# Emptying the finished accumulators at a change of tile: when it is done, and in how many pieces

## The chip, the cores and the metric

One core of a Trainium2 chip. The metric is the device time of one execution in microseconds, the median of the runs. The engines are PE (TensorE), VectorE (DVE in the profile), ScalarE (ACT), GpSimd (POOL) and the DMA queues, SP's above all.

## The reference

```python
w = softmax(weight, axis=-1)             # 8 heads, 7 taps
out[b, s, h, g] = sum_k w[h, k] * x[b, s + k - 6, h, g]   # causal convolution, 24 channels a head
x = out.reshape(16384, 192)
x = (maximum(x @ w_in, 0) ** 2) @ w_out          # layer 1, 192 -> 2048 -> 192
h = x @ w_in2
x = maximum(0.01 * h, h) @ w_out2                # layer 2, 192 -> 2048 -> 192
```

All in float32: 4 x 4096 tokens of 192 channels, a short convolution, and two feed-forward layers one after the other.

## The kernel before

**Tiles and steps.** The 16384 tokens are 32 tiles of 512. A unit (l, t) is layer l on tile t. The units run in the order of `phases` (L297): the pair (1,0) and (1,1) with their steps in turn, then (1,2), (1,3), the pair (2,0) and (2,1), (2,2), (2,3), and from then on, for t = 4, 6, ..., four units: (1,t), (1,t+1), (2,t), (2,t+1). A unit has 8 steps, one for each pair p of 128-column chunks of the 2048; 512 steps in all.

**A step.** PE computes two chunks `h` of the hidden layer (`g1`, L552), ScalarE makes `g` of them by the activation (`act`, L572), in layer 1 one of the two squares is taken on ScalarE and the other on VectorE from step 16 on (`square`, L580), ScalarE casts `g` to a rounded high part `hi` (`high`, L598), VectorE subtracts to get the low part `lo` (`low`, L605), and from step 48 on VectorE also adds the two `lo` of a step to `both` (`add_low`, L611), which saves matmuls. Two steps later (LAG = 2) PE multiplies these with the second weights into accumulators (`g2_one`, L712, through `paired`, L685; for the pairs of tiles `g2`, L631). Matmuls have 64 rows; the two halves of the array run two at a time, each on its own accumulator.

**The accumulators.** 192 output channels in 128-column blocks give a single tile three banks: M (the main 128), F and E, of which half by half the sums are put together: the output's first 128 channels are `M` plus, on one half of the partitions, the other half of `E`, and on the other half the other half of `F`; the last 64 channels are one half of `F` plus the other half of `E`. There are four banks for these (`tags`, L621). The next tile takes the fourth for its M at once, the old E for its F and the old F for its E, so its first matmuls need the old E and F emptied, and the old M only a tile later. In the last step of a tile PE ends E first, then F and M.

**Emptying** (`evac_one`, L732; `evac`, L825, for a pair). `early` (L741) has ScalarE copy E in two copies of 64 partitions, each to the other half: one to `z3`, one to `zs`, a tile of its own. `other` (L746) has ScalarE copy half of F across to `z3`. `add_rest` (L749) adds on VectorE F's other half and `zs`. `add_main` (L752) adds on VectorE M and `z3` on 128 partitions. Then `then` holds what follows three steps on: splitting the sums into the next layer's operand (layer 1), or transposing and storing them (layer 2).

**The order of the work** is written out in a schedule by hand; each engine runs its instructions in the order in which the loop over s (L1160) issues them. In step s PE's part comes first. In step s with p = 1 the last `g2` of the tile before is issued, `leaving` holds the emptying and `alone` is true for a single tile. `early` then stands ahead of the two activations (L1228), `other` and `add_rest` behind the squares (L1268 to L1269), `add_main` at the end (L1280). For a pair all of it stands at the end of the step (L1283).

**Fill.** The convolution (7 taps on VectorE for each 512 tokens and block, L430), decoding the weights (`dec`), splits and transposes (`leave`) are pieces with a cost and a due time. `pieces(s, left)` (L1054) takes them between the step's own instructions: at most `many` a step (2, in layer 1 three, and 1 in the step after a change of tile), and only while `budget` is positive or the piece is due. The budget grows by 3880 a step (4100 before step 48) less the step's own cost, and is at most 4100.

Of the kernel before, what the change touches and what calls it, by code (L numbers as in the profile page):

```python
# [11 lines left out]
I32 = mybir.dt.int32  # L12
# [6 lines left out]
P = 128  # L19
TT = 512  # L20
# [3 lines left out]
LAG = 2  # L24
# [39 lines left out]
def conv_moe_moe2_kernel(  # L64
# [10 lines left out]
    nc = tc.nc  # L75
# [5 lines left out]
    NP = NF // 2  # L81
# [6 lines left out]
    NW = NI + NO  # L88

    const = ctx.enter_context(tc.tile_pool(name="const", bufs=1))  # L90
    stage = ctx.enter_context(tc.tile_pool(name="stage", bufs=1))
# [640 lines left out]
    def evac_one(u):  # L732

        l, t = u
        (M, m_tag), (F, f_tag), (E, e_tag) = ops.pop(u)
        tags.extend([e_tag, f_tag, m_tag])
        v, w = halves(t % 2), halves(1 - t % 2)
        z, z3, zr = ring[:, 0, :], ring[:, 1, :], ring[:, 2, :]
        got = {}

        def early():  # L741
            got["s"] = f32(stage.tile([P, NW], I32, tag="m", name="zs")[:, 0:TT])
            nc.scalar.copy(out=z3[w], in_=E[v])
            nc.scalar.copy(out=got["s"][v], in_=E[w])  # L744

        def other():  # L746
            nc.scalar.copy(out=z3[v], in_=F[w])  # L747

        def add_rest():  # L749
            nc.vector.tensor_add(out=zr[v], in0=F[v], in1=got["s"][v])  # L750

        def add_main():  # L752
            nc.vector.tensor_add(out=z, in0=M, in1=z3)

        if l == 1:
            b, a = splits((2, t), lambda: z, lambda: zr)
            then = [k + ((2, t),) for k in b + a]
        else:
            then = []
            y = y_of(t)  # L760

            def main():
                nc.vector.transpose(out=y()[:, t % 2], in_=z)
                for j in range(4):
                    store(y(), t % 2, j, t, 32 * j)

            def rest():
                nc.vector.transpose(out=y()[:, 2], in_=zr)
                for j in range(4):
                    store(y(), 2, j, t - 1 + j // 2, P + 32 * (j % 2))  # L770

            def rest_alone():
                nc.vector.transpose(out=y()[v, 2], in_=zr[v])
                for j in range(2):
                    store(y(), 2, 2 * (t % 2) + j, t, P + 32 * j)

            then.append((700, main, None, None))
            if t == NT - 2:
                then.append((700, rest_alone, None, None))
            elif t % 2:  # L780
                then.append((700, rest, None, None))
        return (early, other, add_rest, add_main), then

    ys = {}

# [16 lines left out]
    def evac_last(u):  # L802

        l, t = u
        (early, other, add_rest, add_main), _ = evac_one(u)
        early()
        other()
        add_rest()
        add_main()
        v = halves(t % 2)  # L810
        z, zr = ring[:, 0, :], ring[:, 2, :]
        dmas = [nc.sync, nc.scalar]
        y = stage.tile([P, 3, TT], F32, tag="y", name="y").rearrange("p k t -> p (k t)")[:, 0:4 * D].rearrange("p (k d) -> p k d", d=D)
        for i in range(2):
            turned = ps_h.tile([P, TT], F32, tag="h", name="turned")[:, 0:2 * D].rearrange("p (k d) -> p k d", d=D)
            for k in range(2):
                at_ = slice(P * (2 * i + k), P * (2 * i + k + 1))
                nc.tensor.matmul(out=turned[:, k, 0:P], lhsT=z[:, at_], rhs=ident, start=True, stop=True)
                nc.tensor.matmul(out=turned[:, k, P:D], lhsT=zr[v, at_], rhs=ident[v, v], start=True, stop=True)
            w = y[:, 2 * i:2 * i + 2]  # L820
            (nc.vector.tensor_copy if i else nc.scalar.copy)(out=w, in_=turned)
            r0 = t * TT + 2 * P * i
            dmas[i].dma_start(out=out[r0:r0 + 2 * P, :].rearrange("(k t) d -> t k d", t=P), in_=w)

    def evac(u):  # L825

        l, q = u
        o = ops.pop(u)
        tags.extend(tag_of[u][k] for k in ((0, "m"), (1, "m"), (0, "r"), (1, "r")))
        T = [2 * q, 2 * q + 1]  # L830
        z = {}

        def take(i):
            z[i] = ring[:, i, :]
            (nc.vector.tensor_copy if i else nc.scalar.copy)(out=z[i], in_=o[i, "m"])  # L835

        def shift(i):
            if i == 0:
                z["s"], z["r"] = f32(stage.tile([P, NW], I32, tag="m", name="zs")[:, 0:TT]), ring[:, 2, :]
            nc.scalar.copy(out=z["s"][halves(i)], in_=o[i, "r"][halves(1 - i)])  # L840

        def add(i):
            v = halves(i)
            nc.vector.tensor_add(out=z["r"][v], in0=o[i, "r"][v], in1=z["s"][v])

        now = [(0, lambda: take(0)), (690, lambda: take(1))]
        for i in range(2):
            now += [(0, lambda i=i: shift(i)), (690, lambda i=i: add(i))]
        if l == 1:
            then = []  # L850
            for i in range(2):
                b, a = splits((2, T[i]), lambda i=i: z[i], lambda: z["r"])
                then += [p + ((2, T[i]),) for p in a + b]
            return now, then

        y = y_of(2 * q)

        def main(i):
            nc.vector.transpose(out=y()[:, i], in_=z[i])
            for j in range(4):  # L860
                store(y(), i, j, T[i], 32 * j)

        def rest():
            nc.vector.transpose(out=y()[:, 2], in_=z["r"])
            for j in range(4):
                store(y(), 2, j, T[j // 2], P + 32 * (j % 2))

        return now, [(700, lambda: main(0), None, None), (700, lambda: main(1), None, None), (700, rest, None, None)]

    with tc.manual_schedule():  # L870
# [77 lines left out]
        def decode_one():  # L948
            cost, fn = dec.popleft()[1:3]
            fn()  # L950
            budget[0] -= cost
            return cost
# [178 lines left out]
        def needed(s, n):  # L1131

            while n > 0 and dec and dec[0][4] <= s:
                n -= decode_one()
            return n
# [18 lines left out]
            return [g1(u, p), 9]  # L1154

        prep_next = 2
        late = []
        left_at = -2
        going = begin_g1(0)
        for s in range(NS):  # L1160
# [43 lines left out]
            cost = (2100 if vector else 1400) + (700 if three else 0)  # L1204
            budget[0] = max(min(budget[0] + (SHORT if three else STEP) - cost, STEP), DEBT)
            many = MANY[l - 1] + (l == 1 and s >= 4 * NP or 2 * NP - 4 <= s < 2 * NP) if s > 1 else 4
            if left_at == s - 1:
                many = 1
            if leaving:
                left_at = s  # L1210
# [1 line left out]
            if s < 2 * NP:  # L1212
                play(s, A, Z)
                late = [Z]
                if s == 0:
                    split_a((1, 2), third)
                    split_a_lo((1, 2), third)
                continue
            if leaving:
                while leave:  # L1220
                    z = leave.popleft()
                    z[2]()
                    release()
                    budget[0] -= max(z[1], 0)
                while dec and getattr(dec[0][2], "second", False):
                    decode_one()
                if alone:
                    leaving[0]()  # L1228
            left = [many, 1]
            if u in in_pair:  # L1230
                act(*A)
                if late and late[0] not in hi:
                    high(*late[0])
                if not alone:
                    needed(s, 10000)
                    pieces(s, left)
                while leaving and not alone and dec and getattr(dec[0][2], "second", False):
                    decode_one()
                if l == 1:
                    square(*A, False)  # L1240
                if alone:
                    leaving[1]()
                    leaving[2]()
                    leaving[3]()
                    needed(s, 10000)
                    pieces(s, left)
                if late:
                    low(*late.pop())
                high(*A)
# [3 lines left out]
            else:  # L1253
# [5 lines left out]
                act(*one)  # L1259
                act(*two)  # L1260
                needed(s, 10000)
                if not (alone and dec):
                    pieces(s, left, 700)
                if l == 1:
                    square(*Z, vector)
                    square(*A, False)
                if alone:
                    leaving[1]()  # L1268
                    leaving[2]()  # L1269
                pieces(s, left)  # L1270
                while leaving and not alone and dec and getattr(dec[0][2], "second", False):
                    decode_one()
                high(*one)
                high(*two)
                low(*one)
                low(*two)
                if three:
                    add_low(u, p)
                if alone:
                    leaving[3]()  # L1280
                    budget[0] -= 1400
            if leaving and not alone:
                for c, fn in leaving:  # L1283
                    fn()
                    budget[0] -= c
            release()
            if u in in_pair and l == 1:
                square(*Z, vector)
# [40 lines left out]
```

## Time and profile before

| | |
|---|---|
| median of 3 runs | 2165.09 us (2159.32 to 2166.94) |
| the profiled execution | 2162.51 us |
| its span, first to last instruction | 2160.8 us |
| PE busy | 2084.4 us (96% of the span) |
| VectorE busy | 1648.7 us (76%) |
| ScalarE busy | 1478.4 us (68%) |
| GpSimd busy | 60.1 us (3%) |
| mean granted clock of TensorE | 0.995 |

The span is the traced time of one execution; 1.7 us of the execution lie around it. Busy time is the union of an engine's instructions; PE's counts matmuls as pipelined, so its share says little of how far it is from its peak, and the length of a step says more.

### The profile page before, as it was taken

To read this page: it belongs to the slowest core of one execution; us is meant where nothing else is said; L and a number is where in the kernel's file an instruction comes from. 1 tells how busy PE (TensorE), PEld (TensorE's weight loads), DVE (VectorE), ACT (ScalarE), POOL (GpSimd) and SP (SyncE) were. 2 spreads that over 40 slices of the span, in tenths; PEclk is the share of its full clock that TensorE was granted. 3 is DMA by queue.
4 is the path that set the end of the run, shared out by engine and by line. 5 is a ranking of instruction groups with operands and counts; after the bars stand their busy time and mean duration, and the time that the engine had idled before them with its cause. 6 is when DMAs were issued, how large, how long until landed. Compare 5 with 4: busy or idle time off the path is not lost.

```text
span 2160.8 us, 47005 instructions
## 1 busy us (share of the span) xinstructions
PE 2084.4 (96%) x18592; PEld 1974.9 (91%) x18592; DVE 1648.7 (76%) x2575; ACT 1478.4 (68%) x2700; POOL 60.1 (3%) x114
## 2 busy tenths in 40 slices
PE   9899999999999999999999999999999999999998
PEld 6789998999999899998999999999998999989997
DVE  8877678787787877778777787877778777787664
ACT  7877567667676666767667676676767667677674
POOL 2201110000000000000000000000000000000000
PEclk9999999999999999999999999999999999999999
DMA  8540131121212112131121211212121121311110
GB/s 191 137 108 21 27 54 26 39 37 45 37 24 46 29 45 40 21 65 26 36 38 32 50 26 38 37 44 38 24 50 26 45 41 21 64 26 35 25 31 16
DMA packets 232677, 95.07 MB, mean 44 GB/s; under 512 B 203208, under 2 KB 218696, under 8 KB 232456
## 3 DMA queue, kind: packets, MB, share of 16 engines
q1 hardware_dynamic: 229288, 88.90, 21.0%
q0 software_dynamic: 1168, 2.75, 0.6%
q8 instruction: 145, 2.38, 0.5%
q14 instruction: 76, 0.62, 0.1%
q10 hardware_dynamic: 2000, 0.42, 0.1%
HBM read 25.19 MB, written 12.58 MB: 17 GB/s over the span
## 4 chain that ended last, share of the span: by engine, by line
PE 65%; DVE 17%; ACT 11%; issue 5%; DMA 1%; SPq 0%; DVEq 0%; ACTq 0%
PE h L544 31%; PE o1m L544 12%; PE o0r L544 11%; PE o1r L544 7%; DVE lo L607 5%; PE o0m L544 4%; ACT hi L603 2%; DVE g L583 2%; DVE acc_b L435 2%; DVE ring L750 2%; ACT g L576 2%; DVE acc_a L435 2%; ACT ring L747 2%; ACT zs L744 2%; ACT g L578 2%
## 5 line engine op out<-in xcount | busy, mean ns | idle before, releaser
L544 PE MATMUL h<-x,w 64*128 64x512 f32 x9216 | 1362.9, 377 | 2.6 <-ACT g L578 1.4
L544 PEld LDWEIGHTS h<-x,w 64*128 64x128 f32 x9216 | 1067.5, 186 | 13.8 <-ACT g L578 1.8
L607 DVE TENSOR_TENSOR lo<-g,hi 128x512 fp32r<-128x512 f32 x1022 | 661.8, 688 | 347.1 <-ACT hi L603 289.7
L603 ACT CAST hi<-g 128x512 fp32r<-128x512 f32 x1020 | 580.9, 619 | 134.5 <-DVE g L583 130.8
L544 PE MATMUL o1m<-hi,w 64*128 64x512 f32 x2044 | 632.6, 385 | 30.5 <-DVE ring L750 28.7
L544 PE MATMUL o0r<-hi,w 64*128 64x512 f32 x1948 | 601.6, 384 | 17.9 <-DVE ring L750 17.9
L578 ACT ACTIVATE g<-h 128x512 f32<-128x512 f32 x512 | 279.6, 595 | 321.3 <-PE h L544 320.5
L544 PEld LDWEIGHTS o1m<-hi,w 64*128 64x128 f32 x2044 | 358.5, 186 | 59.9 <-DVE ring L750 37.7
L544 PEld LDWEIGHTS o0r<-hi,w 64*128 64x128 f32 x1948 | 342.2, 186 | 47.6 <-DVE ring L750 26.2
L544 PE MATMUL o0r<-lo,w 64*128 64x512 f32 (+1 forms) x1022 | 383.5, 378 | 0.4 <-DVE lo L607 0.4
L576 ACT ACTIVATE g<-h 128x512 f32<-128x512 f32 x512 | 278.6, 593 | 139.9 <-PE h L544 138.1
L544 PE MATMUL o1m<-both,w 64*128 64x512 f32 x926 | 352.4, 381 | 8.1 <-DVE both L619 8.1
L619 DVE TENSOR_TENSOR both<-lo 128x512 fp32r<-128x512 f32 x463 | 320.5, 692 | 18.0
L544 PE MATMUL o0m<-hi,w 64*128 64x512 f32 x1088 | 326.9, 380 | 4.4 <-ACT ring L835 3.2
L544 PE MATMUL o1r<-hi,w 64*128 64x512 f32 x1052 | 321.2, 380 | 1.0 <-ACT zs L744 1.0
L544 PE MATMUL o0m<-lo,w 64*128 64x512 f32 x560 | 209.1, 378 | 0.6 <-DVE lo L607 0.5
L544 PEld LDWEIGHTS o0m<-hi,w 64*128 64x128 f32 x1088 | 191.2, 186 | 9.7 <-ACT ring L835 4.0
L544 PE MATMUL o1r<-lo,w 64*128 64x512 f32 (+1 forms) x526 | 198.0, 376 | 0.0
L544 PEld LDWEIGHTS o1m<-both,w 64*128 64x128 f32 x926 | 172.3, 186 | 19.0 <-DVE both L619 16.8
L544 PEld LDWEIGHTS o0r<-lo,w 64*128 64x128 f32 (+1 forms) x1022 | 187.4, 183 | 2.3 <-issue 0.8
L544 PEld LDWEIGHTS o1r<-hi,w 64*128 64x128 f32 x1052 | 186.6, 186 | 2.4 <-ACT zs L744 1.4
L583 DVE TENSOR_TENSOR g<-g 128x512 f32<-128x512 f32 x243 | 165.6, 682 | 20.1 <-ACT g L576 17.4
(136 smaller groups left out, 1337.6 us busy)
## 6 DMA issues: line engine op xcount, KB each, us to landing
x<-x SPq DMA_DIRECT2D x189, 256.0 KB
out_dram<-y SPq DMA_DIRECT2D x186, 64.0 KB
raw_a<-in_x_dram SPq DMA_DIRECT2D x127, 64.0 KB
raw_b<-in_x_dram SPq DMA_DIRECT2D x62, 64.0 KB
lent<-in_moe_w_out_dram SPq DMA_DIRECT2D x13, 256.0 KB
lent<-in_moe_w_in_dram SPq DMA_DIRECT2D x13, 192.0 KB
lent<-in_moe_w_in_dram SPq DMA_DIRECT2D x13, 128.0 KB
lent<-in_moe_w_out_dram SPq DMA_DIRECT2D x13, 128.0 KB
```

Of the source, the lines that this page charges most:

```text
L435: nc.vector.scalar_tensor_tensor(out=acc[0], in0=src, scalar=w, in1=acc[0], op0=ALU.mult, op1=ALU.add)
L544: return nc.tensor.matmul(out=o.rearrange("p (b a) -> p b a", a=2), lhsT=w, rhs=z.rearrange("p (a b) -> p b a", a=2), start=begin, stop=end_,)
L576: nc.scalar.activation(out=g, in_=hps.pop((u, f)), func=ACTF.Relu)
L578: nc.scalar.activation(out=g, in_=hps.pop((u, f)), func=ACTF.Prelu, alpha=0.01)
L583: nc.vector.tensor_mul(out=g, in0=g, in1=g)
L603: nc.scalar.copy(out=a, in_=gsp[u, f])
L607: nc.vector.tensor_sub(out=b, in0=gsp.pop((u, f)), in1=f32(hi[u, f]))
L619: nc.vector.tensor_add(out=c, in0=f32(lo[u, 2 * p]), in1=f32(lo[u, 2 * p + 1]))
L744: nc.scalar.copy(out=got["s"][v], in_=E[w])
L747: nc.scalar.copy(out=z3[v], in_=F[w])
L750: nc.vector.tensor_add(out=zr[v], in0=F[v], in1=got["s"][v])
```

## The change

`early` becomes one ScalarE copy of E on 128 partitions to `z3`, without changing halves; the tile `zs` is gone. `other` copies F's half to `z` instead of `z3`. `add_rest` adds F's half and `z3`'s other half. `add_main` becomes two additions of 64 partitions: M and `z3` of the other half, then M and `z`. So two VectorE additions now take one input from other partitions than they write.

In the step of the change `early`, `other` and `add_rest` stand at its head, ahead of the activations; for a pair all six operations do. `add_main` moves into `then[0]` and is issued at the end of the step. `both` of the step before a change to another single tile (`soon`) is kept in `pending` and issued behind `add_rest`. In the step of the change `many` is 1, the pieces ahead of the squares are left out, and the budget is charged 1400 for pairs too.

```diff
--- before.py
+++ after.py
@@ -736,21 +736,18 @@
         tags.extend([e_tag, f_tag, m_tag])
         v, w = halves(t % 2), halves(1 - t % 2)
         z, z3, zr = ring[:, 0, :], ring[:, 1, :], ring[:, 2, :]
-        got = {}
-
         def early():
-            got["s"] = f32(stage.tile([P, NW], I32, tag="m", name="zs")[:, 0:TT])
-            nc.scalar.copy(out=z3[w], in_=E[v])
-            nc.scalar.copy(out=got["s"][v], in_=E[w])
+            nc.scalar.copy(out=z3, in_=E)
 
         def other():
-            nc.scalar.copy(out=z3[v], in_=F[w])
+            nc.scalar.copy(out=z[v], in_=F[w])
 
         def add_rest():
-            nc.vector.tensor_add(out=zr[v], in0=F[v], in1=got["s"][v])
+            nc.vector.tensor_add(out=zr[v], in0=F[v], in1=z3[w])
 
         def add_main():
-            nc.vector.tensor_add(out=z, in0=M, in1=z3)
+            nc.vector.tensor_add(out=z[w], in0=M[w], in1=z3[v])
+            nc.vector.tensor_add(out=z[v], in0=M[v], in1=z[v])
 
         if l == 1:
             b, a = splits((2, t), lambda: z, lambda: zr)
@@ -779,7 +776,7 @@
                 then.append((700, rest_alone, None, None))
             elif t % 2:
                 then.append((700, rest, None, None))
-        return (early, other, add_rest, add_main), then
+        return (early, other, add_rest), [add_main] + then
 
     ys = {}
 
@@ -802,11 +799,11 @@
     def evac_last(u):
 
         l, t = u
-        (early, other, add_rest, add_main), _ = evac_one(u)
+        (early, other, add_rest), then = evac_one(u)
         early()
         other()
         add_rest()
-        add_main()
+        then[0]()
         v = halves(t % 2)
         z, zr = ring[:, 0, :], ring[:, 2, :]
         dmas = [nc.sync, nc.scalar]
@@ -843,9 +840,7 @@
             v = halves(i)
             nc.vector.tensor_add(out=z["r"][v], in0=o[i, "r"][v], in1=z["s"][v])
 
-        now = [(0, lambda: take(0)), (690, lambda: take(1))]
-        for i in range(2):
-            now += [(0, lambda i=i: shift(i)), (690, lambda i=i: add(i))]
+        now = [lambda: take(0), lambda: take(1), lambda: shift(0), lambda: add(0), lambda: shift(1), lambda: add(1)]
         if l == 1:
             then = []
             for i in range(2):
@@ -1154,7 +1149,7 @@
             return [g1(u, p), 9]
 
         prep_next = 2
-        late = []
+        late, pending = [], deque()
         left_at = -2
         going = begin_g1(0)
         for s in range(NS):
@@ -1204,7 +1199,7 @@
             cost = (2100 if vector else 1400) + (700 if three else 0)
             budget[0] = max(min(budget[0] + (SHORT if three else STEP) - cost, STEP), DEBT)
             many = MANY[l - 1] + (l == 1 and s >= 4 * NP or 2 * NP - 4 <= s < 2 * NP) if s > 1 else 4
-            if left_at == s - 1:
+            if left_at == s - 1 or leaving:
                 many = 1
             if leaving:
                 left_at = s
@@ -1216,6 +1211,7 @@
                     split_a((1, 2), third)
                     split_a_lo((1, 2), third)
                 continue
+            soon = s + 1 >= LAG and steps[s + 1 - LAG][1] == NP - 1 and steps[s + 1 - LAG][0] not in in_pair
             if leaving:
                 while leave:
                     z = leave.popleft()
@@ -1224,26 +1220,20 @@
                     budget[0] -= max(z[1], 0)
                 while dec and getattr(dec[0][2], "second", False):
                     decode_one()
-                if alone:
-                    leaving[0]()
+                for fn in leaving:
+                    fn()
+                budget[0] -= 1400
+            while pending:
+                pending.popleft()()
             left = [many, 1]
             if u in in_pair:
                 act(*A)
                 if late and late[0] not in hi:
                     high(*late[0])
-                if not alone:
-                    needed(s, 10000)
-                    pieces(s, left)
-                while leaving and not alone and dec and getattr(dec[0][2], "second", False):
-                    decode_one()
+                needed(s, 10000)
+                pieces(s, left)
                 if l == 1:
                     square(*A, False)
-                if alone:
-                    leaving[1]()
-                    leaving[2]()
-                    leaving[3]()
-                    needed(s, 10000)
-                    pieces(s, left)
                 if late:
                     low(*late.pop())
                 high(*A)
@@ -1259,30 +1249,21 @@
                 act(*one)
                 act(*two)
                 needed(s, 10000)
-                if not (alone and dec):
+                if not leaving:
                     pieces(s, left, 700)
                 if l == 1:
                     square(*Z, vector)
                     square(*A, False)
-                if alone:
-                    leaving[1]()
-                    leaving[2]()
                 pieces(s, left)
-                while leaving and not alone and dec and getattr(dec[0][2], "second", False):
-                    decode_one()
                 high(*one)
                 high(*two)
                 low(*one)
                 low(*two)
                 if three:
-                    add_low(u, p)
-                if alone:
-                    leaving[3]()
-                    budget[0] -= 1400
-            if leaving and not alone:
-                for c, fn in leaving:
-                    fn()
-                    budget[0] -= c
+                    (pending.append if soon else lambda fn: fn())(lambda u=u, p=p: add_low(u, p))
+            if alone:
+                then[0]()
+                then = then[1:]
             release()
             if u in in_pair and l == 1:
                 square(*Z, vector)
```

## Rows read from the trace of the kernel before

**Rows 1.** The page's first part: busy time, share of the span, instructions.

```profile
PE 2084.4 (96%) x18592; PEld 1974.9 (91%) x18592; DVE 1648.7 (76%) x2575; ACT 1478.4 (68%) x2700; POOL 60.1 (3%) x114
```

**Rows 2.** Who waited for whom on PE: us in total, times, longest.

```profile
PE o1m L544 <- DVE ring L750: 28.7, 30, 2.4
PE o0r L544 <- DVE ring L750: 17.9, 28, 1.0
```

**Rows 3.** Stretches of one step: length, then PE, PEld, DVE, ACT, POOL busy, PEclk, DMA.

```profile
116.24:120.34 4.10, 4.10 (x42) 3.90 (x39) 3.13 (x6) 3.27 (x6) 0.00 (x0) 1.00 0.63 158
101.43:112.14 10.71, 7.45 (x52) 6.17 (x50) 7.87 (x13) 6.39 (x13) 4.57 (x2) 0.84 0.11 24
140.84:151.24 10.40, 7.05 (x41) 5.50 (x39) 6.68 (x11) 4.99 (x9) 0.68 (x2) 0.69 0.81 212
248.41:257.50 9.09, 7.37 (x50) 6.53 (x48) 4.78 (x8) 4.62 (x10) 2.13 (x6) 0.81 0.16 35
1045.92:1049.81 3.89, 3.89 (x40) 3.89 (x38) 3.59 (x6) 2.58 (x6) 0.00 (x0) 1.00 0.01 2
1041.29:1045.92 4.63, 4.32 (x39) 3.79 (x37) 2.45 (x4) 3.77 (x8) 0.00 (x0) 1.00 0.00 0
974.03:979.32 5.29, 4.32 (x39) 3.79 (x37) 4.04 (x7) 4.19 (x8) 0.00 (x0) 1.00 0.01 3
983.21:988.22 5.01, 4.39 (x40) 3.64 (x37) 4.44 (x7) 3.86 (x8) 0.00 (x0) 1.00 0.17 21
1007.87:1014.04 6.17, 4.57 (x39) 3.71 (x37) 5.29 (x9) 4.94 (x10) 0.00 (x0) 1.00 0.00 0
2023.24:2028.53 5.29, 4.32 (x39) 3.79 (x37) 3.25 (x6) 4.19 (x8) 0.00 (x0) 1.00 0.00 0
```

**Rows 4.** Timeline of the change into (2,14): start us, us, engine, line, operation [idle before].

```profile
1040.48 0.58 ACT L743 COPY ring<-o1m 64x512 f32<-64x512 f32 x1 [1.42 <-PE o1m L544]
...
1041.15 0.38 PE L544 MATMUL o0r<-lo,w 64*128 64x512 f32 x1
...
1041.68 1.08 ACT L578 ACTIVATE g<-h 128x512 f32<-128x512 f32 x2
...
1042.79 0.58 ACT L747 COPY ring<-o0r 64x512 f32<-64x512 f32 x1
...
1042.88 0.38 PE L544 MATMUL o1m<-both,w 64*128 64x512 f32 x1
...
1043.40 0.70 DVE L750 TENSOR_TENSOR ring<-o0r,zs 64x512 f32<-64x512 f32 x1 [2.73 <-ACT ring L747]
...
1044.15 0.48 PE L544 MATMUL o0r<-hi,w 64*128 64x512 f32 x1 [0.31 <-DVE ring L750]
```

**Rows 5.** Timeline of VectorE after the change into (1,14) and at that into (1,15).

```profile
981.03 0.69 DVE L753 TENSOR_TENSOR ring<-o1r,ring 128x512 f32<-128x512 f32 x1
...
982.39 0.65 DVE L583 TENSOR_TENSOR g<-g 128x512 f32<-128x512 f32 x1
983.73 1.29 DVE L607 TENSOR_TENSOR lo<-g,hi 128x512 fp32r<-128x512 f32 x2 [0.69 <-ACT hi L603]
985.05 0.69 DVE L619 TENSOR_TENSOR both<-lo 128x512 fp32r<-128x512 f32 x1
...
1008.76 0.69 DVE L619 TENSOR_TENSOR both<-lo 128x512 fp32r<-128x512 f32 x1
```

**Rows 6.** Lines of ScalarE and VectorE (busy us, mean ns | idle), and two timeline rows.

```profile
L835 ACT COPY ring<-o0m 128x512 f32<-128x512 f32 x2 | 1.2, 578 | 0.0
...
L410 DVE COPY xT_a<-xT_a 128x6 f32<-128x6 f32 x26 | 4.4, 168 | 0.0
...
L413 DVE COPY xT_b<-xT_b 64x6 f32<-64x6 f32 x16 | 2.6, 164 | 0.6
...
107.33 0.67 DVE L844 TENSOR_TENSOR ring<-o1r,zs 64x512 f32<-64x512 f32 x1
108.03 0.69 DVE L844 TENSOR_TENSOR ring<-o0r,zs 64x512 f32<-64x512 f32 x1
```

## The prediction

> **What bounds the kernel now.** I read the page's first part, then who waited for whom on PE, then step lengths, then the order of work around three changes of tile. PE is busy 96% of the span, VectorE 76%, ScalarE 68% [rows 1]: TensorE is the bound, and what can be won is where it stands still. Its two longest waits by far are 28.7 and 17.9 us, 58 times in all, both for line 750, `add_rest` [rows 2]. So at a change the last bank to come free is F, the one that `add_rest` reads.
>
> A wait's idle time is not its price, since one half of the array runs alone before it and it restarts slowly. The price is the length of the step. A quiet step of the stage with `both` takes 3.89 us, one before it 4.10 [rows 3]. The step after a change takes: into a layer-2 tile 4.63 (0.74 too long); into an even layer-1 tile (here 14) 5.29 (1.40), with a second stall of 1.12 two steps on (5.01); into an odd one (15) 6.17 (2.28) [rows 3]. Three early changes, two of them next to a pair of tiles, cost 10.71, 10.40 and 9.09 us: 6.61 + 6.30 + 5.20 = 18.1 too long, with a mean granted clock of 0.84, 0.69 and 0.81, so part of each ran at the lower of the clock's two levels (1.2 instead of 2.4 GHz) after PE had stood idle; the late steps show 1.00 [rows 3].
>
> How often: 29 single tiles are changed to in layer 2, 14 even and 14 odd ones in layer 1 (tiles 4 to 31), the last round (30, 31) without the taps of a following pair: there 1.40 at both changes (5.29 again [rows 3]) and no second stall. All of it: 29 x 0.74 = 21.5; 14 x 1.40 + 13 x 1.12 = 34.2; 13 x 2.28 + 1.40 = 31.0; with the early 18.1 that is 105 us.
>
> **The change, part by part.** I follow one change into layer 2 [rows 4], with S = 1041.29, the start of the step in which the banks are wanted.
> - E is copied once (128 partitions) instead of twice (64 each): a 128x512 copy takes 0.58 us, and so does a 64x512 one, so ScalarE saves 0.58 us a change [rows 4, 6].
> - The copy of F moves from behind the two activations to ahead of them. F's last matmul starts at 1041.15 and ends at 1041.53, S + 0.24, so the copy can run 1041.55 to 1042.13 instead of 1042.79 to 1043.37. It is a wait put at the head of ScalarE's queue: the activations behind it go from 1041.68 to 1042.15, 0.45 later, and the casts behind them no longer have the copy ahead. PE wants none of this before the step after; it costs nothing there.
> - `add_rest` needs E's copy and F itself: 1041.57 to 1042.28 instead of 1043.40 to 1044.10. PE stood 0.31 us for the bank, with one half already running alone, and went on at 1044.15. This wait goes, on every tile.
> - What is late next: the sum `both` of the step before (0.69 us) is moved behind `add_rest` on VectorE's queue, 1042.30 to 1043.00. An even tile reads it in the third pair of matmuls, which started at 1042.88: a new stall of some 0.15 us, 0.25 with the restart. An odd tile reads it a third of the step later: none. So layer 2 wins 0.74 on 15 odd tiles and 0.5 on 14 even ones: 11.1 + 7.0 = **18.1 us** (bounds: 0 on even tiles if the new stall is as long as the old, 0.74 if PE finds it in time: 11 to 21).
> - `add_main` becomes two adds of 64 partitions, in place of one of 0.69 us. VectorE's add of 64 partitions takes as long as one of 128 (0.70 against 0.69) [rows 4, 5]; two in turn on different halves follow at 0.70 us [rows 6], where two on the same partitions, 1.29 together, follow at 0.60 [rows 5]. So VectorE gets 0.70 us more a change, 60 times 0.70 = 42 us; in layer 2 it idles and this is hidden.
> - The number of fill pieces in the step of the change falls to 1. In layer 1 it was 3. The budget keeps what it didn't spend, so the two convolution taps (0.75 us each) come back in the third and fourth step of the tile.
>
> The last two matter in **layer 1**, where VectorE is the second bound. After the change into tile 14 its queue runs `both`, `add_main`, a transpose, the square (982.39), the wait for the casts, two `lo`, `both` at 985.05 to 985.74 [rows 5]; that last is what PE stood for in the step that began at 983.21. From there each step ends on VectorE. With the change, worked down the same queue from S = 974.03: `add_rest` 974.3, `both` 975.0 to 975.7 (PE loses 0.2), square to 976.3, one tap to 976.95, `lo` to 978.6, `both` 979.2, two adds 980.6, transpose 981.25, square 981.9, casts, `lo` 983.85, `both` 984.5. PE, which no longer stood 1.40, wants that one at 983.6: stalls 0.2 + 1.0 in place of 2.5. PE is 1.25 ahead, of which the two taps that come back take about 0.5 in the next steps: 0.8 us is kept. Into the odd tile, from S = 1007.87: the `lo` end at 1008.75 as they do now (`both` follows there [rows 5]), `add_rest` 1009.45, `both` 1010.2, square 1010.9, tap 1011.5, `lo` 1012.9, `both` 1013.6. The bank stall of 2.28 is gone, so PE's next step starts at S + 3.89 = 1011.76 and its third pair, 1.59 later (1042.88 - 1041.29 [rows 4]), wants that sum at 1013.35: 0.3 back. Then the two adds to 1014.95, square 1015.6, casts and `lo` 1017.55, `both` 1018.25 in time, a split, and so to a `both` at 1022.15 that is wanted at 1021.4: 0.8 back. 1.2 kept. So a round of two keeps 2.0 of 4.8: 13 x 2.05 = **26.7 us** (bounds 0, if VectorE's queue takes all, and 13 x 4.8 = 62). The last round has no taps: 1.15 + 1.40 = **2.6 us**.
>
> Early: the copies out of the pair's banks, and their additions, go from the end of the step to its head. PE's idle time was the whole of ScalarE's and VectorE's step ahead of them; what is left is the drain itself, 0.58 on ScalarE beside 0.67 to 0.70 on VectorE [rows 6], partly under the next tile's h matmuls, and a later activation. I leave 2.6 of the 18.1 us for the three: **15.5 us** (bounds 9, half of it, and 18), the lower clock gone with the long idle. DMA issues are not moved, SP's and POOL's queues are not passed.
>
> Sum: 18.1 + 26.7 + 2.6 + 15.5 = 62.9. The profiled execution took 2162.5 (span 2160.8): 2099.6. The median of the runs shown is 2.6 above it, so I say 2102.
>
> **The rivals.**
> - VectorE's queue is no limit in layer 1, all stalls go: 105 less, 2162.5 - 105 = 2058, 2060 by the median. For: VectorE is idle a quarter of the span. Against: the 5.01 us step, ended by `both`, with VectorE busy 4.44 of it [rows 3]. 0.14.
> - The new wait takes the old one's place in layer 1: the later `both`, the second add and the returned taps eat all that the bank gives, and even layer-2 tiles keep their stall: 11.1 + 2.6 + 12 = 26 less, 2137, with the median 2139. For: the same 5.01 us step. Half this way (layer 1 nothing, the rest as forecast) gives 2129. 0.14.
> - Slower: adding across partitions is dear. `add_rest` and the first half of `add_main` now take an SBUF input from the other 64 partitions; the trace has VectorE doing that only in a 64x6 copy, 164 ns, against 168 for a 128x6 copy in place [rows 6]: no surcharge, but six columns. If each of the two adds took d longer, 28 layer-1 changes would pay 2d, 14 even layer-2 ones d, 15 odd ones d - 0.45: 85d - 7. That eats the 63 at d = 0.8, and makes the kernel over 0.3% slower from d = 0.9 on, an add of 1.6 instead of 0.69 us; at three times the present duration (d = 1.38) it is 47 us slower, 2212. 0.05. The Trainium skill (VectorE: DVE Perf Modes, "Why `tensor_reduce` can't reduce along partition axis") speaks against such adds: each lane is an independent pipeline with no path across lanes. By it the halves would have to be moved first, which is this rival; the trace's copy across the halves doesn't bear it out for a plain shift of the start partition.
>
> **How the numbers follow.** Forecast 0.64, all stalls gone 0.14, given back 0.14, dear additions 0.05, a mixture that ends near no change 0.03. Within 0.3% (6.5 us, about what a measurement of this kernel can tell from no change) is only the last: faster 0.92, same 0.03, slower 0.05. Range: the forecast's bounds (layer 2: -7, +3; layer 1: -27, +35; early: -6, +3) together don't all fall one way; I take 2068 to 2138, which holds the forecast's case, most of the given-back one, and not the case without any stall nor the slow one.
>
> **What would show it.** Right: PE no longer waits for `add_rest`; its first wait after an even change is for `both`, some 0.1 to 0.2 us; layer-2 steps after a change of 3.9 (odd) and 4.1 us (even); granted clock 1.00 in the three early stretches; in even layer-1 tiles a step of about 5 us two steps after the change that still ends on `both`; the adds of lines with crossed inputs at 0.68 to 0.70 us. Wrong: a crossed add well over 0.7 us; the even tile's `both` stall near 1 us; no second stall in layer 1 (then nearer 2060); or ScalarE's activations making PE wait for h banks.

## The result and the profile after

The changed kernel takes 2141.49 us (median of 4 runs, 2140.63 to 2141.95), the kernel before beside it 2163.84: a ratio of 0.9898 [0.9879, 0.9917]. It is faster by 22 us, where 63 were forecast; 2141 lies above the range. The span falls from 2160.8 to 2138.9 us.

The page's first part and the engines of its chain, to be held against [rows 1]:

```profile
PE 2083.2 (97%) x18592; PEld 1951.9 (91%) x18592; DVE 1686.7 (79%) x2635; ACT 1439.5 (67%) x2640; POOL 68.2 (3%) x114
...
PE 63%; DVE 25%; ACT 5%; issue 5%; DMA 1%; SPq 1%; DVEq 0%; POOL 0%
```

VectorE has 60 instructions and 38 us more, ScalarE 60 and 39 us less: one addition in, one copy out at each of 60 changes. Who waited for whom on PE, against [rows 2]:

```profile
PE o1m L544 <- DVE both L619: 33.9, 80, 0.6
PE o1r L544 <- DVE lo L607: 6.0, 1, 6.0
```

The wait for the bank, 46.6 us in 58 waits, is gone (`add_rest`, now line 746, is waited for once, 0.6 us). In its place stand 80 waits for `both`, 33.9 us, and one long one. The kernel before had 13 waits for `both`:

```profile
PE o1m L544 <- DVE both L619: 8.1, 13, 0.6
```

The steps, against [rows 3] (same columns): two early changes, (2,15), (2,14), (1,14) and its second stall, three steps of (1,15), and a step of (2,3).

```profile
99.33:104.52 5.19, 5.19 (x52) 4.89 (x50) 4.47 (x8) 4.44 (x9) 0.76 (x2) 1.00 0.01 3
...
232.83:237.84 5.01, 5.01 (x49) 4.75 (x47) 3.11 (x5) 3.66 (x7) 1.33 (x5) 1.00 0.01 3
...
1056.71:1060.61 3.90, 3.90 (x39) 3.75 (x37) 2.92 (x5) 3.26 (x6) 0.00 (x0) 1.00 0.00 0
...
1024.69:1029.46 4.77, 4.30 (x40) 3.72 (x37) 3.60 (x6) 3.14 (x6) 0.00 (x0) 1.00 0.00 0
957.60:962.38 4.78, 4.31 (x40) 3.73 (x37) 3.84 (x6) 3.83 (x7) 0.00 (x0) 1.00 0.02 3
966.26:971.13 4.87, 4.31 (x40) 3.73 (x37) 4.43 (x7) 3.72 (x8) 0.00 (x0) 1.00 0.17 22
...
995.41:999.85 4.44, 4.23 (x39) 3.59 (x37) 4.36 (x7) 1.99 (x4) 0.00 (x0) 1.00 0.00 0
999.85:1004.46 4.61, 4.48 (x39) 3.48 (x37) 3.34 (x6) 3.79 (x7) 0.00 (x0) 1.00 0.00 0
1004.46:1009.15 4.69, 4.23 (x41) 3.59 (x38) 3.84 (x7) 4.05 (x9) 0.00 (x0) 1.00 0.45 100
...
272.88:285.51 12.63, 6.60 (x39) 5.17 (x37) 6.62 (x10) 2.69 (x7) 1.64 (x3) 0.73 0.40 79
```

Early, 10.71 and 9.09 became 5.19 and 5.01 at full clock. An odd layer-2 tile's step fell from 4.62 to 3.90, a quiet step. An even one's rose, 4.63 to 4.77. Into (1,15) the one step of 6.17 became three long ones in a row (4.44, 4.61, 4.69).

By units (first h matmul of one to that of the next): up to the start of (2,3) 19.6 us were won (276.9 to 257.3); (2,3) itself lost 7.6 (32.3 to 39.9); the 13 odd layer-2 tiles from 5 to 29 won 9.2 (31.88 to 31.16 each in the mean), the 14 even ones lost 1.7 (31.88 to 32.00); all of layer 1 from tile 4 on won 2.2. But for some 0.1 in the last unit and in rounding that is the whole difference of the spans, 21.9.

**The new stall of the even tiles.** Timeline of the change into (2,14), S = 1024.69, against [rows 4]:

```profile
1023.88 0.58 ACT L740 COPY ring<-o1m 128x512 f32<-128x512 f32 x1 [1.42 <-PE o1m L544]
...
1024.95 0.58 ACT L743 COPY ring<-o0r 64x512 f32<-64x512 f32 x1 [0.49 <-PE o0r L544]
...
1025.57 0.69 DVE L746 TENSOR_TENSOR ring<-o0r,ring 64x512 f32<-64x512 f32 x1 [2.30 <-ACT ring L743]
...
1026.29 0.69 DVE L619 TENSOR_TENSOR both<-lo 128x512 fp32r<-128x512 f32 x1
...
1027.04 0.48 PE L544 MATMUL o1m<-both,w 64*128 64x512 f32 x1 [0.47 <-DVE both L619]
```

`add_rest` does not start when F is complete (S + 0.26) but when the copy of F ends (S + 0.84): 0.6 later than forecast. `both`, queued behind it, is 0.6 later too, and PE stands 0.47 us for it.

**Layer 1.** VectorE in (1,15), two steps after the change, against [rows 5]:

```profile
998.67 0.73 DVE L435 SCALAR_TENSOR_TENSOR acc_a<-xT_a,taps,acc_a 128x512 f32<-128x512 f32 x1
999.33 0.68 DVE L583 TENSOR_TENSOR g<-g 128x512 f32<-128x512 f32 x1
1000.69 1.29 DVE L607 TENSOR_TENSOR lo<-g,hi 128x512 fp32r<-128x512 f32 x2 [0.69 <-ACT hi L603]
1002.02 0.69 DVE L619 TENSOR_TENSOR both<-lo 128x512 fp32r<-128x512 f32 x1
1002.63 0.68 DVE L484 TENSOR_TENSOR x<-ring,x 64x512 fp32r<-64x512 f32 x1
1003.23 0.68 DVE L583 TENSOR_TENSOR g<-g 128x512 f32<-128x512 f32 x1
1004.59 1.29 DVE L607 TENSOR_TENSOR lo<-g,hi 128x512 fp32r<-128x512 f32 x2 [0.69 <-ACT hi L603]
```

Each step VectorE takes a piece (a tap, a split), then its square, then stands 0.69 us until ScalarE has cast that square. From one square to the next are 3.90 us (999.33 to 1003.23), as long as a quiet step of PE: a lag at the change is never made up, while every few steps something more is queued.

**The one-off stall.** The fifth step of (2,3): VectorE, SP's queue, and PE; then the stretch after it in the form of [rows 3].

```profile
278.72 0.71 DVE L760 STREAM_TRANSPOSE y<-ring 128x512 f32<-128x512 f32 x1 [7.58 <-DMA x<-x]
...
240.35 33.04 SPq L794 DMA_DIRECT2D out_dram<-y  x12
...
280.66 0.79 PE L544 MATMUL o1r<-lo,w 64*128 64x512 f32 x1 [6.03 <-DVE lo L607]
```

```profile
280.00:285.00 5.00, 4.34 (x20) 3.50 (x22) 4.90 (x9) 0.52 (x2) 1.13 (x3) 0.50 0.21 30
```

The transpose of tile 2 writes the buffer `y`, and the 12 output stores of the pair (0,1) are still reading it. (Its row names the transfers of `x`, issued behind the stores, as what came last; the row of before, below, names the stores.) SP's queue is issuing them from 240.35 to 273.39, and the transpose starts 5.3 us after that. The same stood in the kernel before, 5.2 us from the last issue (287.99) to the transpose, but there the transpose was wanted 20.4 us later (291.5, not 271.1) and the stores only 14.6, so that it waited 1.67:

```profile
254.91 33.08 SPq L797 DMA_DIRECT2D out_dram<-y  x12
...
293.18 0.71 DVE L763 STREAM_TRANSPOSE y<-ring 128x512 f32<-128x512 f32 x1 [1.67 <-DMA out_dram<-y]
```

**The crossed additions.** All instructions of lines 746, 749 and 750, by source line: duration ns min/median/max.

```profile
L746 DVE TENSOR_TENSOR ring<-o1m,ring x30: 682/682/684, 135.1 to 2099.3; 64x512 f32<-64x512 f32 x30
L746 DVE TENSOR_TENSOR ring<-o0r,ring x29: 694/694/695, 305.8 to 2127.3; 64x512 f32<-64x512 f32 x29
...
L749 DVE TENSOR_TENSOR ring<-o0m,ring x30: 694/695/696, 138.8 to 2102.9; 64x512 f32<-64x512 f32 x30
...
L750 DVE TENSOR_TENSOR ring<-o0m,ring x30: 682/683/684, 139.5 to 2103.6; 64x512 f32<-64x512 f32 x30
```

Lines 746 and 749 read their second input from the other 64 partitions, 750 does not; all take 0.68 to 0.70 us.

### The profile page after: what moved, and what is told of

Its sections match the earlier page's. It is cut to its first block, busy times and chain, and to the rows that moved or that the text cites. A ratio compares the mean times of both kernels' runs of the same rounds, so it can differ in the third digit from the quotient of the medians.

```text
span 2138.9 us, 46835 instructions
## 1 busy us (share of the span) xinstructions
PE 2083.2 (97%) x18592; PEld 1951.9 (91%) x18592; DVE 1686.7 (79%) x2635; ACT 1439.5 (67%) x2640; POOL 68.2 (3%) x114
## 3 DMA queue, kind: packets, MB, share of 16 engines
q0 software_dynamic: 1168, 2.75, 0.7%
## 4 chain that ended last, share of the span: by engine, by line
PE 63%; DVE 25%; ACT 5%; issue 5%; DMA 1%; SPq 1%; DVEq 0%; POOL 0%
PE h L544 30%; PE o1m L544 11%; PE o0r L544 10%; DVE lo L607 7%; PE o1r L544 7%; DVE both L619 5%; PE o0m L544 4%; DVE g L583 4%; ACT hi L603 3%; DVE acc_a L435 2%; DVE acc_b L435 1%; DVE ring L746 1%; ACT ring L743 1%; DVE ring L750 1%; DVE ring L749 1%
## 5 line engine op out<-in xcount | busy, mean ns | idle before, releaser
L544 PEld LDWEIGHTS h<-x,w 64*128 64x128 f32 x9216 | 1041.9, 186 | 18.5 <-DVE x L480 1.2
L544 PE MATMUL o1m<-hi,w 64*128 64x512 f32 x2044 | 620.7, 381 | 0.6 <-DVE ring L746 0.6
L544 PE MATMUL o0r<-hi,w 64*128 64x512 f32 x1948 | 586.6, 379 | 0.0
L544 PE MATMUL o1m<-both,w 64*128 64x512 f32 x926 | 359.8, 389 | 34.9 <-DVE both L619 33.9
L585 ACT ACTIVATE g<-g 128x512 f32<-128x512 f32 x269 | 169.1, 631 | 7.8
```

The source lines that it names most:

```text
L544: return nc.tensor.matmul(out=o.rearrange("p (b a) -> p b a", a=2), lhsT=w, rhs=z.rearrange("p (a b) -> p b a", a=2), start=begin, stop=end_,)
L585: nc.scalar.activation(out=g, in_=g, func=ACTF.Square)
```

## The experiments

Five theories for the missing 41 us: `add_rest` waits for F's copy and `both` waits behind it; layer 1 has too much fill, or has it in the wrong place; the early transpose meets the stores; the new forms cost more than they save. All edits are to the changed kernel, except where one says otherwise; "the kernel before" ran beside each and took 2162 to 2164 us.

**1. `add_rest` ahead of F's copy.**

```diff
+                if alone:
+                    leaving[0]()
+                    leaving[2]()
+                    leaving[1]()
```

> Issues add_rest ahead of the copy of F at single tiles, all else as in the changed kernel (2141.5 us). Theory A (the wait for the copy is only the order in which two readers of one bank are issued): add_rest starts about 0.6 us earlier in the step, at S + 0.3, the sum both behind it too, the even layer-2 step after a change falls from 4.77 to about 4.15, and the copy of F starts behind add_rest. About 9 us less in layer 2 and up to 8 in layer 1: 2125 to 2133. Rival B (add_rest needs something of the copy, or VectorE itself is late): add_rest starts where it did and the time is the same, or up to 5 us longer because the activations stand behind a later copy.

Measured 2151.33, ratio 0.9954 [0.9937, 0.997]: 10 us slower than the change. Timeline of the change into (2,14), S = 1030.90:

```profile
1031.24 0.69 DVE L746 TENSOR_TENSOR ring<-o0r,ring 64x512 f32<-64x512 f32 x1 [1.76 <-PE o0r L544]
...
1031.97 0.58 ACT L743 COPY ring<-o0r 64x512 f32<-64x512 f32 x1 [1.29 <-DVE ring L746]
1032.57 1.09 ACT L578 ACTIVATE g<-h 128x512 f32<-128x512 f32 x2
```

The addition now starts as soon as F is there, and the copy waits for it: the two never lie side by side, whichever is issued first. They read different halves of F and write different rows of `ring`; no run separates the two tensors. But the changed kernel's trace has ScalarE and VectorE write different rows of `ring` at the same time, at a change from a pair, where they read different banks:

```profile
100.61 0.59 ACT L832 COPY ring<-o0m 128x512 f32<-128x512 f32 x1 [0.65 <-PE o0m L544]
...
100.67 0.69 DVE L832 COPY ring<-o1m 128x512 f32<-128x512 f32 x1 [0.18 <-PE o1m L544]
```

So `ring` alone does not make the order, which leaves the common bank; whether the program's own waits or the chip keep it there is not shown. The Trainium skill (PSUM — Partial Sum Buffer, "Terms") keeps two engines apart in one bank per 32-partition quadrant, by which the two halves could be read together; no run here shows that they can. The step of this even tile falls to 4.23 (4.77), so the theory of the stall holds. But the activations start at S + 1.67 instead of S + 0.87, and layer 1 pays: (1,14) has a step of 5.78 (4.87) and PE a new wait for ScalarE's cast, 7.3 us in 14 waits.

**2. `both` in its old place.**

```diff
-                    (pending.append if soon else lambda fn: fn())(lambda u=u, p=p: add_low(u, p))
+                    add_low(u, p)
```

> Leaves the sum both where the step before has it, instead of behind add_rest. Theory A (the moved sum is the wait that took the place of the old one at even tiles, and VectorE idles in front of add_rest while the sum stands behind it): even layer-2 step 4.77 to 3.9, 14 x 0.87 = 12 us less; in layer 1 the even tile's first stall of 0.9 goes and VectorE's queue is 0.7 shorter, 0.5 to 1 us a round, 7 to 14 less; in all 2115 to 2122. Rival B (layer 1 is bound by ScalarE's copies at the head of its queue): the 12 us of layer 2 alone, 2129. Rival C (the move was needed to let add_rest run early): odd tiles get a stall for the bank, and the time is 2140 or more.

Measured 2120.59, 0.9811 [0.9796, 0.9826]: 21 us won. Steps into (2,14) and the second stall of (1,14):

```profile
1017.84:1021.74 3.90, 3.90 (x40) 3.75 (x38) 2.07 (x4) 3.14 (x6) 0.00 (x0) 1.00 0.00 0
959.12:964.44 5.32, 4.65 (x40) 3.64 (x37) 4.57 (x8) 4.00 (x8) 0.00 (x0) 1.00 0.16 20
```

The deferral alone cost an even layer-2 tile 0.87 us. VectorE had stood 2.30 us ahead of `add_rest`; the 0.69 us of the sum fit there and delay nothing. In layer 1 the first stall goes as well, half of it into the second (5.32 from 4.87).

**3. One piece of fill a step in all of layer 1.**

```diff
-            if left_at == s - 1 or leaving:
+            if left_at == s - 1 or leaving or l == 1 and s >= THREE:
```

> At most one fill piece in every step of layer 1 from step 48 on (three before), the rest goes to layer 2, where VectorE idles. Theory A (in layer 1 VectorE's queue is the bound, with the taps): the layer-1 units fall from 33.6 to about 31.5 to 32.3, the even ones keeping their first stall of 0.9, 28 units, 35 to 55 us less: 2087 to 2106. Rival B (the chain through ScalarE's activations and casts binds): layer-1 units stay at 33.5, within 5 us of 2141. Rival C (the pieces come due and are forced in the last layer-2 steps): the stall moves there, the gain is under 20.

Measured 2131.52, 0.9861 [0.9846, 0.9876]. Ten us, far less than expected: (1,15) keeps its 4.45, 4.54 and 4.69, and only the last stall of (1,14) goes. As long as it stands ahead of the squares, its amount is not what binds (number 7 takes the same edit with the fill behind them).

**4. The transpose of tile 2 held back to the sixth step after its change of tile, instead of the third.**

```diff
-            then.append((700, main, None, None))
+            then.append((700, main, (lambda at=now[0]: now[0] >= at + 6) if t == 2 else None, None))
```

> Holds back the output transpose of tile 2 (layer 2) by three steps, so that it comes after the pair's 12 output stores have left the one y buffer. Theory A (that transpose at the head of VectorE's queue is what the 12.63 us step of unit (2,3) waits for): that step falls to about 3.9 to 5, 2132 to 2134. Rival B (the stores hold up more than that, the copies of x behind them too): another instruction of VectorE or PE waits as long, less than 3 us won.

Measured 2131.92, 0.9864 [0.9849, 0.9878]: 9.6 us won, and the step of 12.63 is a quiet one, clock 1.00:

```profile
274.33:278.23 3.90, 3.90 (x39) 3.75 (x37) 3.79 (x7) 2.72 (x6) 0.61 (x2) 1.00 0.21 22
```

**5. Layer-1 fill behind the square.** The same pieces, none ahead of the squares.

```diff
-                if not leaving:
+                if not leaving and l == 2:
                     pieces(s, left, 700)
```

> In layer 1 no fill piece is taken ahead of the squares any more; all of them come behind the square on VectorE, where VectorE otherwise stands 0.69 us a step until ScalarE has cast that square. All else as in the changed kernel (2141.5). Theory A (in layer 1 VectorE's queue in its order binds: square, the gap of 0.69, two lo, both, piece: 3.92 us a step with a piece ahead of the square, 3.31 with the piece in the gap, against PE's 3.89): the steps of 4.4 to 4.7 in odd tiles go to about 3.9 to 4.2, the layer-1 units from 33.6 to about 32.2, 28 units, 2095 to 2117. Rival B (only the amount of VectorE's work counts, not where it stands): within 5 us of 2141.

Measured 2109.90, 0.9755 [0.9738, 0.9773]: 32 us won, the most of any single edit to the change. VectorE in (1,15):

```profile
987.93 0.67 DVE L583 TENSOR_TENSOR g<-g 128x512 f32<-128x512 f32 x1
988.53 0.74 DVE L435 SCALAR_TENSOR_TENSOR acc_a<-xT_a,taps,acc_a 128x512 f32<-128x512 f32 x1
989.29 1.29 DVE L607 TENSOR_TENSOR lo<-g,hi 128x512 fp32r<-128x512 f32 x2
990.62 0.69 DVE L619 TENSOR_TENSOR both<-lo 128x512 fp32r<-128x512 f32 x1
991.23 0.68 DVE L583 TENSOR_TENSOR g<-g 128x512 f32<-128x512 f32 x1
```

The tap lies in the 0.69 us in which VectorE stood; from square to square it is now 3.30 us instead of 3.90, and a lag is made up in a step or two. (1,15) takes 31.7 us instead of 33.4, its long steps 4.23, 3.93, 4.09.

**6. Edits 2, 4 and 5 together; 7. and edit 3 with them.**

> The sum both in place (that alone 2120.6), tile 2's transpose held back (that alone 9.6 us less) and the pieces of layer 1 behind the square. Theory A: the two known gains add to 2111, and the gap takes 1 to 1.7 us more from each of 28 layer-1 units: 2065 to 2085. Rival B (place of the pieces without effect): 2111.

> As the run before it, with at most one piece a step in layer 1. Theory A: every layer-1 step has VectorE at 3.31 to 3.4 us, below PE's 3.89, so lag is made up at once and almost every step takes 3.9: 2055 to 2075, a little below the run before it. Rival B (the pieces come due and are forced ahead of a unit's first step): above it.

Measured 2083.29, 0.9631 [0.9613, 0.9648], and 2068.40, 0.9564 [0.9549, 0.9579]. The single edits are worth 21 + 10 + 32 = 62; together they give 58. So the three causes are nearly separate. With one piece a step as well it is 15 us less, and one stall is left: 0.8 us in each even layer-1 tile, two steps after the change.

**8. The old forms of the emptying at the new places.** On edit 2: E in two copies, one addition for M.

```diff
-            nc.vector.tensor_add(out=z[w], in0=M[w], in1=z3[v])
-            nc.vector.tensor_add(out=z[v], in0=M[v], in1=z[v])
+            nc.vector.tensor_add(out=z, in0=M, in1=z3)
```

> The sum both in place (2120.6), with the emptying's old forms at the new places: E in two copies of 64 partitions across the halves, one addition of 128 partitions for M, no addition with inputs from other partitions. ScalarE has 0.58 us more at a change, VectorE 0.70 less. Theory A (VectorE's queue binds layer 1): 0.3 to 0.6 less at each of 28 layer-1 changes, 2104 to 2114. Rival B (ScalarE's place at the head of the step binds, as the run with add_rest first showed when activations went 0.7 later): 2120 to 2135.

Measured 2104.69, 0.973 [0.9714, 0.9745], 16 us less than edit 2. The second addition for M is VectorE time in layer 1 (the stall in (1,14) falls from 5.32 to 4.61). At these places the copy of E saved in exchange is worth nothing: layer-2 units take 31.1 us with either form.

**9. The new forms alone at the old places** (on the kernel before: the diff's first hunk without the moves).

> The kernel before with one part of the change alone: E in one copy of 128 partitions, the additions across partitions, M in two additions, all at the old places (kernel before 2162). Theory A (VectorE's queue in layer 1 pays 0.70 for the second addition; ScalarE's 0.58 less lets activations, the copy of F and add_rest come up to 0.58 earlier, so the old bank wait shrinks by up to that): layer-2 changes 4.63 to about 4.1, 15 us less; layer 1 between 0.5 better and 0.5 worse a unit; 2135 to 2160. Rival B (crossed additions are dear in themselves): an addition over 0.75 us and a time above 2162.

Measured 2129.90, 0.984 [0.9825, 0.9854]: 34 us won, more than by the whole change. The change into (2,14), S = 1027.75:

```profile
1028.54 0.58 ACT L743 COPY ring<-o0r 64x512 f32<-64x512 f32 x1
...
1029.15 0.69 DVE L746 TENSOR_TENSOR ring<-o0r,ring 64x512 f32<-64x512 f32 x1 [2.02 <-ACT ring L743]
```

```profile
1027.75:1031.67 3.92, 3.92 (x39) 3.77 (x37) 2.45 (x4) 2.95 (x6) 0.00 (x0) 1.00 0.00 0
```

Behind one copy instead of two everything on ScalarE comes earlier: F's copy starts at S + 0.79, not S + 1.50 [rows 4], `add_rest` with it, and the whole stall of a layer-2 tile, even or odd, is gone without any move.

**10. The pairs' emptying alone at the head of the step** (on the kernel before).

```diff
+                else:
+                    for c, fn in leaving:
+                        fn()
+                        budget[0] -= c
...
-            if leaving and not alone:
-                for c, fn in leaving:
-                    fn()
-                    budget[0] -= c
```

> The kernel before with the emptying of the pairs of tiles moved to the head of the step, nothing else. The two pair changes (10.71 and 9.09 us, both partly at the lower clock) fall to about 5.2 and 5.0 as in the changed kernel: 9 to 10 us less, 2150 to 2154, if the early gain comes from this move. Rival: the early gain of 20 us came from the single tiles' change and the wait passes on: within 4 us of 2162.

Measured 2163.52, 0.9998 [0.9986, 1.0009]: nothing. The step into (2,2) and the fifth of (2,3):

```profile
241.97:246.99 5.02, 5.02 (x50) 4.77 (x48) 3.05 (x5) 3.67 (x7) 1.34 (x6) 1.00 0.02 4
282.95:294.43 11.48, 6.27 (x38) 4.84 (x36) 5.08 (x8) 2.43 (x6) 0.79 (x3) 0.70 0.67 123
```

Both pair changes are short now (5.31 and 5.02), and the gain goes into the same transpose: 4.16 before, 11.48 now.

**11. Edits 2 to 5 with the old forms; 12. and `add_main` of layer 1 behind the next step's square.**

> The run with one piece a step behind the square, both in place and tile 2's transpose held back (2068.4), now with the emptying's old forms (two copies of E, one addition for M). Theory A: the one stall left in layer 1, 0.83 in even tiles two steps after the change, loses the 0.70 of the second addition: 14 x 0.7 = 10 less, 2056 to 2061. Rival B: ScalarE's second copy gives it back, 2066 or more.

> As the run before it, and in layer 1 the addition for M stands behind the next step's square, in the gap in which VectorE waits for ScalarE's cast, instead of ahead of it. Theory A (what stands in the gap is hidden): no stall left at a change, 0 to 5 us less than the run before it, 2051 to 2058. Rival B: no difference beyond 1 us, since the addition's place isn't on the path any more.

Measured 2053.91, 0.9494 [0.948, 0.9508], and 2054.29, 0.9494 [0.948, 0.9509]: the fastest version, and a last move that adds nothing. Page and step (1,14) that had been the second stall, in number 11:

```profile
PE 2038.0 (99%) x18592; PEld 1966.9 (96%) x18592; DVE 1651.9 (81%) x2575; ACT 1464.4 (71%) x2700; POOL 63.6 (3%) x114
```

```profile
930.50:934.41 3.91, 3.91 (x40) 3.76 (x37) 3.81 (x7) 3.05 (x6) 0.00 (x0) 1.00 0.15 20
```

From tile 4 to the last step but one every step but one (4.24, in (1,4)) takes 3.88 to 3.91 us; PE waits neither for `add_rest` nor for `both`. The change's moves are kept here, its forms and its deferral are not: 110 us less than before.

## Why the prediction was right and wrong

Of the 41 us that are missing, 27 are layer 1's, 10 those of layer 2 from tile 4 on and 8 those of (2,3); the early part gave 4 more than forecast.

- **Right: the sign, the odd layer-2 tiles, the early part.** An odd tile's step fell by 0.72 (0.74 forecast). The three early steps of 10.71, 10.40 and 9.09 became 5.19, 5.13 and 5.01, 14.9 us for 15.5, at clock 1.00, and the 80 waits on `both` are the next late thing it named. That 19.6 us were won up to (2,3) is in part luck: 2.6 of them come from the change from (1,3) into the pair of layer 2 (its step of 8.73 became 6.15), which the prediction did not count. And at the two pairs the move alone does it (5.31 and 5.02, number 10), but at (1,3) the 10.40 fell to 6.02 with the new forms alone (number 9) and to 9.38 in number 10, without them.
- **Wrong: "`add_rest` needs E's copy and F itself".** It also starts only when F's copy has ended. [Rows 4] show it, 1043.40 behind a copy that ends at 1043.37 and named there as the releaser; I took that for the order of the queues. So `both` is 0.6 later than walked, an even layer-2 tile loses 0.12 where 0.5 should have been won (18.1 became 7.5 us from tile 4 on, with the odd tiles), and each even layer-1 tile stalls 0.9 in the step after the change (0.2 forecast).
- **Wrong: the walk down VectorE's queue in layer 1**, 26.7 us for 13 rounds, measured 2.4 (and the last round −0.2 for 2.6). (Its own 0.8 and 1.2 a round give 26.0; it multiplied by 2.05.) In the even tile it began with the same 0.6. In (1,15) it had the tap behind the square, in VectorE's wait for the casts, and it charged the pieces that come back 0.5 us a round. In the trace a tap and two splits stand ahead of the squares there, and the three long steps are 2.1 us over quiet ones in sum, where 1.1 was forecast. Number 5 shows what the place of the fill is worth: 32 us with the same fill. So the late part went the way of the second rival, the new wait in the old one's place (2139): its later `both`, its second addition and the fill are what numbers 2, 8 and 5 show, 21 (part of it in layer 2), 16 and 32 us. That its time is nearly the measured one is luck in part: its 12 us for the early steps came about as 19.6 less the 7.6 lost in (2,3), a stall that it didn't have.
- **Wrong: "SP's and POOL's queues are not passed".** VectorE's work was moved past SP's: the transposes came earlier, the 33 us of stores ahead of them did not get shorter. 8.7 us, shown by numbers 4 and 10.
- **Mis-sized: the copy saved on ScalarE, put at nothing beside the moves.** At the old places the new forms alone win 34 us (number 9), since F's copy and so `add_rest` stand behind the copy that is saved; the sum had no term for this.
- **The rival of dear crossed additions falls**: d, the surcharge, is under 0.02 us.

Against the forms alone (number 9), the moves win 14.7 us up to (2,3) (272.0 to 257.3), lose 4.2 in it (35.7 to 39.9), and from tile 4 on lose 0.83 on each even layer-2 tile (31.17 to 32.00) and 0.66 on each odd layer-1 tile (32.81 to 33.46 in the mean). So in part the change works against itself: the copy it saves already cured in layer 2 what its moves were to cure, and with the moves it is 12 us slower than without. The other losses are the second addition and fill that stands ahead of the squares, as it did before the change.

## What to carry to other kernels

Before moving an instruction, read what released it in the trace, not only what its operands need: here the second of two readers of a bank waited for the first, in either order of issue. On an engine that works in order and goes to and fro with another, where a piece of fill stands counts for more than how much there is: put it into the gap of the round trip. And whoever moves work earlier should look up what frees its buffers, down to the store queue.

## What the hardware showed that was not expected

- A VectorE addition with one input from the other 64 partitions costs what one in place does, 682 to 696 ns in 120 cases. The Trainium skill (VectorE: DVE Perf Modes, "Why `tensor_reduce` can't reduce along partition axis") says, of reductions along the partitions, that there is no path across lanes. These additions reduce nothing and only take an input that starts 64 partitions away, and that had no price here; the rival read more into that section than it states.
- SP's queue took 33.0 us to issue twelve output stores of 64 KB, 2.75 each, and 4.15 us for three transfers of 256 KB behind them.
- After PE had stood 6.0 us its clock was granted at 0.50, the lower of the two levels, for the 5 us that follow; pairs of matmuls started 0.43 us apart there (282.10, 282.53, 282.95), and 0.22 apart at full clock.
